# Strassen's seven products in the second product of a fused attention and feed-forward kernel, with masks of four rows moved to GpSimd

## The chip, the cores and the metric

The kernel runs on one core of a Trainium2 chip. The metric is the device time of one execution in microseconds (us), as the median of several runs. A profiled execution comes with a trace of every instruction; its span goes from the first to the last of them.

## The reference

Attention over 8 batch rows, 8 heads, 576 positions and 64 values a head. Four heads see a sliding window of 32 positions, four see every fourth position of the last 128. Its output, 4608 tokens of 512 values, goes through a feed-forward layer:

```python
scores = np.where(masks[None, :, :, :], scores, -1000000000.0)
scores = scores - np.max(scores, axis=-1, keepdims=True)
attn = np.exp(scores)
attn = attn / (np.sum(attn, axis=-1, keepdims=True) + 1e-09)
return np.matmul(attn, v).astype(np.float32)
...
h = x @ w_in
r = np.maximum(h, 0.0)
g = r * r
return (g @ w_out).astype(np.float32)
```

w_in is 512 x 2048, w_out 2048 x 512. Inputs and output are float32; the kernel's matmuls take float16.

## The kernel before, in words

"Row" below is a batch row b (0 to 7), "chunk" is 512 of the 4608 tokens (c = 0 to 8). A chunk needs the attention output of the row with its number and the one before.

*Feed-forward.* The first product (`mm1_tile`, L254) makes one tile of the hidden layer at a time: 128 hidden features by the chunk's 512 tokens, four matmuls (L262) into one PSUM bank. ScalarE takes relu into a tile `rt` of four buffers (L247), VectorE squares it into `g` (L251): 16 tiles a chunk. The second product (`mm2_gen`) has the weights in `g` (128 x 128) and w_out as the moving operand, 512 columns wide: 16 matmuls for each of four groups of 128 tokens (L292), then a copy by ScalarE (L302) and a store from SP's queue (L303). `g` has two buffers, one per chunk. Chunk 0's first product also computes the last 64 tokens of row 0 for chunk 1, so that its second half is 288 columns wide and chunk 1's tiles 448.

*Attention.* Scores (L415 sliding, L429 dilated) go into PSUM pairs, ScalarE takes exp into `AT` (L402), VectorE multiplies by a 0/1 mask (L404). The values product (AV: L470, L484) is normalized by VectorE out of PSUM (L455, L456), transposed by TensorE (L499, L517) and copied by ScalarE into `xT` (L505, L523), a ring of four rows' tokens.

*Loads.* GpSimd's queue loads q and k: `n` (L140) and `dd` (L216). GpSimd copies `n` into token order, `o` (L223); SP stores it to DRAM as `dp` (L229) and loads `dd` and `dp` back transposed into QKTd and QKTp (L241, L237). SP loads v into `sv` and `sd` (L150, L158, L160), and GpSimd casts them to float16 as `vp`, `vd` (L195, L199). `see` (L181) is a one-element copy that makes GpSimd wait for the transposes of a row before it issues the next loads.

*Order.* It is written out by hand. The feed-forward of chunk b - 1 is a generator; the attention of row b calls `pump(n)`, which emits n steps of it. A tile of the first product is two steps; before, the second product has eight steps per group of tokens. For rows 2 to 7 the order before is: `see`, q and k loads for row b + 1, the copy to token order, the transposes, `cast_v`, `load_v` for row b + 1, `pump(24)`, then `attn_scores` with `pump(4)` after each of four scores, then `attn_values` with `pump(2)` after each piece, then the rest of the chunk. Chunks 7 and 8 come after the last row with no attention between. Eight PSUM banks: four (`bank`) are turned over by feed-forward tiles and transposes, four are the two pairs of the attention.

The line numbers in the profile of before are those of the listing.

Of the kernel before, what the change touches and what calls it, by code (L numbers as in the profile page):

```python
# [17 lines left out]
def kernel(  # L18
# [38 lines left out]
    wpool = ctx.enter_context(tc.tile_pool(name="wpool", bufs=1))  # L57
    stg = ctx.enter_context(tc.tile_pool(name="stg", bufs=1))
    natp = ctx.enter_context(tc.tile_pool(name="natp", bufs=2))
    xp = ctx.enter_context(tc.tile_pool(name="xp", bufs=4))  # L60
    gp = ctx.enter_context(tc.tile_pool(name="gp", bufs=2))
    osb = ctx.enter_context(tc.tile_pool(name="osb", bufs=4))
    pspool = ctx.enter_context(tc.tile_pool(name="pspool", bufs=1, space=bass.MemoryType.PSUM))
    dpool = ctx.enter_context(tc.tile_pool(name="dpool", bufs=2, space=bass.MemoryType.DRAM))
# [37 lines left out]
    def w_out_of(ffc):  # L102
        return wo[ffc // 4][:, ffc % 4, :]

    QKTp = [const.tile([P, 2, 2, PADP + S], FP16, name=f"QKTp{r}") for r in range(2)]
    QKTd = [const.tile([P, 2, 2, KPAD + S], FP16, name=f"QKTd{r}") for r in range(2)]
    AT = const.tile([P, 8, 640], FP16, name="AT")
# [27 lines left out]
            )  # L135

    def load_whole_sliding_qk(b):
        n = natp.tile([P, HH, 9, D], FP16, name=f"n{b}", tag="n")
        for i, s in ((1, k), (0, q)):
            nc.gpsimd.dma_start(  # L140
                out=n[64 * i : 64 * (i + 1)],
                in_=s[b, 0:HH].rearrange("h (p j) d -> p h j d", j=9),
            )
        return n
# [97 lines left out]

    def relu_squared(ph, w, outs, name):
        rt = osb.tile([P, TOKC], FP16, name=name, tag="rt")
        nc.scalar.activation(rt[:, 0:w], ph[:, 0:w], ACTF.Relu)  # L247
        o = 0
        for g in outs:
            n = g.shape[1]  # L250
            nc.vector.tensor_mul(g, rt[:, o : o + n], rt[:, o : o + n])  # L251
            o += n

    def mm1_tile(name, ffc, t0, t1, outs):  # L254
        w = t1 - t0
        ph = bank()
        o = t0 % RING
        cut = min(w, RING - o)
        for dmk in range(NDM):
            for a, b, x in ((0, cut, o), (cut, w, 0)):  # L260
                if a < b:
                    nc.tensor.matmul(  # L262
                        ph[:, a:b],
                        w_in_of(dmk, ffc),
                        xT[:, dmk, x : x + b - a],
                        start=(dmk == 0 and a == 0),
                        stop=(dmk == NDM - 1 and b == w),
                    )
            if dmk == 1:
                yield  # L270
        relu_squared(ph, w, outs, f"rt{name}")
        yield

    def mm1_first_gen(g0, g1):

        for f4 in range(0, NFF, 4):
            for ffc in range(f4, f4 + 4):
                yield from mm1_tile(f"0_{ffc}_0", ffc, 0, HALF, [g0[:, ffc, 0:HALF]])
            for ffc in range(f4, f4 + 4):
                yield from mm1_tile(  # L280
                    f"0_{ffc}_1", ffc, HALF, S, [g0[:, ffc, HALF:TOKC], g1[:, ffc, 0:REST]]
                )

    def mm1_gen(c, g):
        o = REST if c == 1 else 0
        for ffc in range(NFF):
            yield from mm1_tile(
                f"{c}_{ffc}", ffc, c * TOKC + o, (c + 1) * TOKC, [g[:, ffc, o:TOKC]]
            )

    def mm2(c, g, po, t, ffc):
        nc.tensor.matmul(  # L292
            po,
            g[:, ffc, t * P : (t + 1) * P],
            w_out_of(ffc),
            start=(ffc == 0),
            stop=(ffc == NFF - 1),
        )
# [3 lines left out]
        nc.scalar.copy(ot, po)  # L302
        nc.sync.dma_start(out=out[(c * 4 + t) * P : (c * 4 + t + 1) * P, :], in_=ot)  # L303

    def mm2_gen(c, g):
        for t in range(TOKC // P):
            po = bank()
            for ffc in range(NFF):
                mm2(c, g, po, t, ffc)
# [5 lines left out]
    def mm2_by_rows_gen(c, g):  # L315
        pos = [
            bank() for t in range(TOKC // P)
        ]
        for f4 in range(0, NFF, 4):
            for t, po in enumerate(pos):  # L320
                for ffc in range(f4, f4 + 4):
                    mm2(c, g, po, t, ffc)
# [6 lines left out]
    def hidden(c):  # L329
        return gp.tile([P, NFF, TOKC], FP16, name=f"g{c}", tag="g")  # L330

    hid = {}

    def moe_gen(c):
        g = hid.pop(c) if c in hid else hidden(c)
        yield from mm1_gen(c, g)
        yield from mm2_gen(c, g)
# [63 lines left out]
    def softmax(u, ps, mask, eng=nc.vector):  # L401
        nc.scalar.activation(AT[:, u, 0:UW], ps[:, :, 0 : UW // 2], ACTF.Exp, scale=scale)  # L402
        if mask is not None:
            eng.tensor_mul(AT[:, u, 0:UW], AT[:, u, 0:UW], mask)  # L404
# [39 lines left out]
    def s_dilated(b, a):  # L444
        tiles = [pair() for t in range(2)]
        for t, ps in enumerate(tiles):
            s_dilated_one(b, a, t, ps)
        for t, ps in enumerate(tiles):
            softmax(4 + 2 * a + t, ps, maskd)

    def normalize(b, what, pav, w):
        x = xp.tile([QB, 2, HH, D], FP16, name=f"x{b}_{what}", tag="x")
# [72 lines left out]
            py[:, 0:UW].rearrange("x (c r i) -> x c i r", c=2, r=DIL),  # L525
        )

    def attn_scores(b, gap):
        for hp in range(2):
            s_sliding(b, hp)  # L530
            pump(gap)
        for a in range(2):
            s_dilated(b, a)
            pump(gap)

    def attn_values(b, gap, wide=False):
        xs = []
        for mp in range(3):
# [18 lines left out]


    ns0 = [stg.tile([P, 2, 9 * D], FP16, name=f"ns0_{hp}") for hp in range(2)]
    nd0 = natp.tile([P, 36 * D], FP16, name="nd0", tag="nd")  # L560
# [121 lines left out]
    xs = [av_sliding(0, mp) for mp in range(2)]  # L682
    x_dilated(0, 0, ys, True)
    x_sliding(0, 0, xs, True)
    g0, g1 = hidden(0), hidden(1)
    hid[1] = g1
    pairs[:] = [2, 3]
    pending.append(mm1_first_gen(g0, g1))
    pump(2)
    zs = [av_dilated(0, 1, 0)]  # L690
    pump(2)
# [5 lines left out]
    x_sliding(0, 1, xs, True)  # L697
    k_pads(1)
    v_ones(1)
    ns1 = natp.tile([P, HH, 9 * D], FP16, name="ns1", tag="n")  # L700
    nd1 = natp.tile([P, 36 * D], FP16, name="nd1", tag="nd")
    for i, src in ((1, k), (0, q)):
        nc.gpsimd.dma_start(
            out=ns1[64 * i : 64 * (i + 1)],
# [19 lines left out]
    o = in_token_order(2, n)  # L724
    transpose_dilated(2, dd)
    transpose_sliding(2, keep_sliding_qk(2, o))
    pending.append(mm2_by_rows_gen(0, g0))
    pump(4)
    t_sliding(1, ns1, 0)
    pump(2)  # L730
# [64 lines left out]
```

## Time and profile before

| what | value |
|---|---|
| median of 3 runs | 318.48 us (318.02 to 320.24) |
| the profiled execution's own time | 317.65 us |
| its span | 315.5 us |
| mean granted clock of TensorE | 0.993 |
| copy of an output tile by ScalarE (L302) | 0.585 us each, 36 of them |
| masks on VectorE (L404) | 56, mean 581 ns (dilated) and 486 ns (sliding) |
| a row and its chunk in the middle, 94.75 to 127.11 us of the span | 32.36 us |
| a chunk with no attention, 256.70 to 284.33 us | 27.63 us |

A line of a group reads: line of the kernel, engine, operation, what it writes <- what it reads, shapes, count | busy us in total, mean ns of one | idle us of the engine before it, and what ended the idle time. PE is TensorE's matmuls, PEld its weight loads, DVE VectorE, ACT ScalarE, POOL GpSimd. In a timeline: start and length in us, engine, line, operation, count of instructions merged into the line, and in brackets the idle time before them. In a line of a window: its bounds and length, then busy us and count of PE, PEld, DVE, ACT and POOL, the granted clock of TensorE, the DMA share and GB/s.

### The profile page before, as it was taken

What the parts mean: (1) busy time and instruction counts of PE and PEld (TensorE: products, weight loads), DVE (VectorE), ACT (ScalarE), POOL (GpSimd) and SP (SyncE); (2) the same over time, 40 slices, a digit from 0 to 9 for tenths busy, and PEclk for the clock granted to TensorE, in tenths of its full rate; (3) what the DMA queues carried; (4) which work ended last, traced back from release to release, by engine and by line L of the source; (5) the groups of instructions that cost most, each with busy time, mean ns of one, the idle gap of its engine ahead of it and who ended that gap; (6) DMA issues with size and microseconds to landing.
All of it is one profiled execution on the core that took longest, in us unless ns stands there. A gap on an engine that the chain in (4) does not pass through costs nothing.

```text
span 315.5 us, 6596 instructions
## 1 busy us (share of the span) xinstructions
PE 303.0 (96%) x2628; PEld 174.7 (55%) x2628; DVE 160.6 (51%) x378; ACT 170.7 (54%) x301; POOL 77.4 (25%) x120
## 2 busy tenths in 40 slices
PE   4988999999999999999999999999999999999995
PEld 3657945565455555555589555555554555445542
DVE  7456757547734974586435652575256524203400
ACT  2647855578336843684368535763577256316611
POOL 5492017203602903533422440040000000000000
PEclk9989999999999999999999999999999999999999
DMA  6999979689979999999978965781100110010011
GB/s 117 235 196 212 214 163 241 139 217 221 202 189 219 273 182 211 292 185 190 239 202 183 191 171 136 169 198 55 68 2 2 66 69 1 31 69 35 0 66 66
DMA packets 72782, 46.69 MB, mean 148 GB/s; under 512 B 54384, under 2 KB 65904, under 8 KB 72560
## 3 DMA queue, kind: packets, MB, share of 16 engines
q1 hardware_dynamic: 65504, 32.65, 42.5%
q0 software_dynamic: 7248, 13.63, 24.4%
q8 instruction: 20, 0.33, 0.4%
q14 instruction: 10, 0.08, 0.1%
HBM read 39.85 MB, written 16.52 MB: 179 GB/s over the span
## 4 chain that ended last, share of the span: by engine, by line
PE 88%; DMA 5%; SPq 1%; POOL 1%; ACT 1%; DVE 1%; issue 1%; POOLq 0%; DVEq 0%
PE PS L292 38%; PE PS L262 38%; PE PS L484 3%; DMA sv<-in_v_dram 3%; DMA ns<-in_q_dram 2%; PE PS L470 2%; PE PS L415 2%; PE PS L429 1%; PE PS L499 1%; PE PS L517 1%; SPq L150 1%; DVE x_p L456 1%; PE PS L359 1%; POOL ns L125 1%; PE PS L408 0%
## 5 line engine op out<-in xcount | busy, mean ns | idle before, releaser
L292 PE MATMUL PS<-wo,g 128*128 128x512 f16 x576 | 140.5, 379 | 0.0
L262 PE MATMUL PS<-xT,wi 128*128 128x512 f16 (+3 forms) x704 | 130.3, 343 | 1.5 <-ACT xT L505 1.5
L251 DVE TENSOR_TENSOR g<-rt 128x512 f16<-128x512 f16 (+4 forms) x176 | 71.8, 421 | 91.4 <-ACT rt L247 89.3
L247 ACT ACTIVATE rt<-PS 128x512 f16<-128x512 f32 (+2 forms) x160 | 88.8, 556 | 33.9 <-PE PS L262 31.4
L262 PEld LDWEIGHTS <-wi 128*128 128x128 f16 x704 | 78.5, 114 | 46.6 <-issue 0.9
L292 PEld LDWEIGHTS <-g 128*128 128x128 f16 x576 | 49.8, 97 | 46.5
L302 ACT COPY ot<-PS 128x512 f32<-128x512 f32 x36 | 21.1, 585 | 51.7 <-PE PS L292 51.7
L402 ACT ACTIVATE AT<-PS 128x576 f16<-128x576 f32 x64 | 38.3, 650 | 8.6 <-PE PS L429 5.7
L505 ACT COPY xT<-PS 128x576 f16<-128x576 f16 x16 | 10.2, 639 | 28.7 <-PE PS L499 28.7
L199 POOL CAST vd<-sd 128x512 f16<-128x512 f32 x32 | 20.3, 662 | 13.1 <-DMA sd<-in_v_dram 13.0
L195 POOL CAST vp<-sv 128x512 f16<-128x512 f32 x24 | 16.4, 696 | 28.0 <-DMA sv<-in_v_dram 27.6
L456 DVE TENSOR_TENSOR x_d<-PS,rcp_d 72x512 f16<-72x512 f32 x32 | 22.0, 686 | 1.1
L223 POOL COPY o<-n 128x2304 f16<-128x2304 f16 x6 | 12.8, 2136 | 28.9 <-DMA n<-in_q_dram 28.9
L404 DVE TENSOR_TENSOR AT<-AT,maskd 128x576 f16<-128x576 f16 x28 | 15.7, 581 | 6.1 <-ACT AT L402 4.6
L456 DVE TENSOR_TENSOR x_p<-PS,rcp_p 96x512 f16<-96x512 f32 x24 | 16.5, 686 | 0.8
L455 DVE RECIPROCAL rcp_d<-PS 72x8 f32<-72x8 f32 x32 | 6.5, 202 | 20.3 <-PE PS L484 19.6
L484 PEld LDWEIGHTS <-AT 128*128 128x128 f16 x256 | 12.5, 101 | 7.6 <-DVE x_d L456 0.8
L404 DVE TENSOR_TENSOR AT<-AT,maskp 128x576 f16<-128x576 f16 x28 | 13.5, 486 | 4.4 <-ACT AT L402 2.2
L523 ACT COPY xT<-PS 128x576 f16<-128x576 f16 x16 | 10.2, 639 | 8.9 <-PE PS L517 8.9
L484 PE MATMUL PS<-vd,AT 128*128 128x65 f16 x256 | 14.0, 199 | 0.0
L470 PEld LDWEIGHTS <-AT 128*128 128x128 f16 x192 | 9.6, 102 | 6.3 <-issue 1.2
L181 POOL COPY look<-QKTp 1x1 f16<-1x1 f16 x5 | 1.2, 232 | 48.1 <-DMA QKTp<-dp 48.1
(63 smaller groups left out, 132.2 us busy)
## 6 DMA issues: line engine op xcount, KB each, us to landing
out_dram<-ot SPq DMA_DIRECT2D x36, 256.0 KB, 2.6
sv<-in_v_dram SPq DMA_DIRECT2D x40, 128.0 KB, 4.5
sd<-in_v_dram SPq DMA_DIRECT2D x8, 512.0 KB, 9.9
dp<-o SPq DMA_DIRECT2D x12, 288.0 KB, 3.8
sd<-in_v_dram SPq DMA_DIRECT2D x8, 288.0 KB
wo<-in_moe_w_out_dram POOLq DMA_DIRECT2D x4, 512.0 KB, 13.2
n<-in_k_dram POOLq DMA_DIRECT2D x6, 288.0 KB, 5.3
n<-in_q_dram POOLq DMA_DIRECT2D x6, 288.0 KB, 6.8
```

The source lines that it names most:

```text
L195: nc.gpsimd.tensor_copy(vp[b % 2][:, m : m + 2, :, 0:D], sv[:, m : m + 2, :, :])
L199: nc.gpsimd.tensor_copy(vd[b % 2][:, t, c : c + 2, :, 0:D], sd[:, t, :, D * c : D * (c + 2)].rearrange("p h (c d) -> p c h d", d=D),)
L247: nc.scalar.activation(rt[:, 0:w], ph[:, 0:w], ACTF.Relu)
L251: nc.vector.tensor_mul(g, rt[:, o : o + n], rt[:, o : o + n])
L262: nc.tensor.matmul(ph[:, a:b], w_in_of(dmk, ffc), xT[:, dmk, x : x + b - a], start=(dmk == 0 and a == 0), stop=(dmk == NDM - 1 and b == w),)
L292: nc.tensor.matmul(po, g[:, ffc, t * P : (t + 1) * P], w_out_of(ffc), start=(ffc == 0), stop=(ffc == NFF - 1),)
L302: nc.scalar.copy(ot, po)
L402: nc.scalar.activation(AT[:, u, 0:UW], ps[:, :, 0 : UW // 2], ACTF.Exp, scale=scale)
L404: eng.tensor_mul(AT[:, u, 0:UW], AT[:, u, 0:UW], mask)
L456: nc.vector.tensor_tensor(out=x[0:w], in0=pv[:, :, :, 0:D], in1=rcp[0:w].unsqueeze(3).to_broadcast([w, 2, HH, D]), op=ALU.mult,)
L470: nc.tensor.matmul(pav[:, i, h * (D + 2) : h * (D + 2) + D + 1], AT[:, 2 * (h // 2) + m // 3, off : off + P], vp[b % 2][:, m, h, 0 : D + 1 ...
L484: nc.tensor.matmul(pav[:, e, h * (D + 2) : h * (D + 2) + D + 1], AT[:, 4 + 2 * a + t, off : off + P], vd[b % 2][:, t, 2 * a + e, h, 0 : D ...
```

## The change

For chunks 2 to 8 the second product is done by Strassen's scheme in Winograd's form. `g` and w_out are cut into quarters; seven products of quarters, each 2 x 8 matmuls with 256 columns, fill one PSUM bank each. VectorE makes four sums of quarters of `g` (S1 to S4) while the first product goes on, two hidden features of each half at a time, and seven additions out of PSUM; GpSimd makes four sums of quarters of w_out (T1 to T4) once. Stores go out by quarters of 256 tokens by 256 values. The tiles of the first product are taken in the order 0, 8, 1, 9, ..., 7, 15. `g` has one buffer, chunk 0 no longer computes for chunk 1, and `n` has one buffer; nd shares its buffers with `o`. The masks of rows 4 to 7 are done by GpSimd. In the loop over rows the copy to token order, the transposes and the loads of v come after the scores; `cast_v` comes after the scores in rows 2 and 3; other counts go to `pump`. A Strassen product is four steps.

```diff
-    gp = ctx.enter_context(tc.tile_pool(name="gp", bufs=2))
+    n1p = ctx.enter_context(tc.tile_pool(name="n1p", bufs=1))
...
+    g = wpool.tile([P, NFF, TOKC], FP16, name="g")
+    HF = NFF // 2
+    HT = TOKC // 2
+    S1, S2, S3, S4 = (wpool.tile([P, HF, HT], FP16, name=f"S{i}") for i in range(1, 5))
+    T1, T2, T3, T4 = (wpool.tile([P, HF, HT], FP16, name=f"T{i}") for i in range(1, 5))
...
-        n = natp.tile([P, HH, 9, D], FP16, name=f"n{b}", tag="n")
+        n = n1p.tile([P, HH, 9, D], FP16, name=f"n{b}", tag="n")
...
+    def sum_w_out(upper):
+
+        for j in range(2):
+            f = slice(4 * j, 4 * j + 4)
+            b11, b12 = wo[j][:, :, 0:HT], wo[j][:, :, HT:DM]
+            b21, b22 = wo[2 + j][:, :, 0:HT], wo[2 + j][:, :, HT:DM]
+            if upper:
+                nc.gpsimd.tensor_sub(T1[:, f, :], b12, b11)
+            else:
+                nc.gpsimd.tensor_sub(T3[:, f, :], b22, b12)
+                nc.gpsimd.tensor_sub(T2[:, f, :], b22, T1[:, f, :])
+                nc.gpsimd.tensor_sub(T4[:, f, :], b21, T2[:, f, :])
+
+    def first_quarters(j):
+        f = slice(j, j + 2)
+        nc.vector.tensor_sub(S3[:, f, :], g[:, f, 0:HT], g[:, f, HT:TOKC])
+
+    def all_quarters(j):
+        f, h = slice(j, j + 2), slice(HF + j, HF + j + 2)
+        nc.vector.tensor_add(S1[:, f, :], g[:, f, HT:TOKC], g[:, h, HT:TOKC])
+        nc.vector.tensor_sub(S2[:, f, :], S1[:, f, :], g[:, f, 0:HT])
+        nc.vector.tensor_sub(S4[:, f, :], g[:, h, 0:HT], S2[:, f, :])
+
+    def mm1_sums_gen(c):
+        for j in range(HF):
+            for ffc in (j, HF + j):
+                yield from mm1_tile(f"{c}_{ffc}", ffc, c * TOKC, (c + 1) * TOKC, g[:, ffc, :])
+                if j % 2 == 1:
+                    (first_quarters if ffc == j else all_quarters)(j - 1)
+                yield
+
+    def product(po, lhs, rhs):
+        for t in range(2):
+            for j in range(HF):
+                nc.tensor.matmul(
+                    po[:, HT * t : HT * (t + 1)],
+                    lhs(j)[:, t * P : (t + 1) * P],
+                    rhs(j),
+                    start=j == 0,
+                    stop=j == HF - 1,
+                )
+                if j == 3:
+                    yield
+            if t == 0:
+                yield
+
+    def seven_gen(c):
...
+        po = bank()
+        yield from product(po, a(0, 0), b(0, 0))
+        s1 = new("s1", "s1")
+        nc.scalar.copy(s1, two(po))
+        yield
+        p7 = bank()
+        yield from product(p7, s(S3), s(T3))
+        yield
+        po = bank()
+        yield from product(po, s(S2), s(T2))
+        u2, t7 = new("u2", "u2"), new("t7", "t7")
+        nc.vector.tensor_add(u2, two(po), s1)
+        nc.vector.tensor_add(t7, two(p7), u2)
+        yield
+        po = bank()
+        yield from product(po, a(0, 1), b(1, 0))
+        c11 = new("c11", "ot")
+        nc.vector.tensor_add(c11, two(po), s1)
+        keep(0, 0, c11)
...
-    def s_sliding(b, hp):
+    def s_sliding(b, hp, eng=nc.vector):
...
-            softmax(2 * hp + half, ps, maskp)
+            softmax(2 * hp + half, ps, maskp, eng)
...
     for b in range(2, B):
-        pending.append(moe_gen(b - 1))
+        pending.append(moe_gen(b - 1) if b == 2 else moe_seven_gen(b - 1))
+        eng = nc.vector if b < 4 else nc.gpsimd
         if b + 1 < B:
             see(QKTp[b % 2][0:1, 0, 0, PADP : PADP + 1])
             n, dd = load_whole_sliding_qk(b + 1), keep_dilated_qk(b + 1)
+        if b > 3:
+            cast_v(b)
+        pump({2: 24, 3: 12}.get(b, 8))
+        s_sliding(b, 0, eng)
+        pump(4 if b == 2 else 6)
+        s_sliding(b, 1, eng)
+        pump({2: 4, 3: 6}.get(b, 8))
+        s_dilated(b, 0, eng)
+        pump({2: 4, 3: 6}.get(b, 8))
+        s_dilated(b, 1, eng)
+        if b < 4:
+            cast_v(b)
+        if b + 1 < B:
             o = in_token_order(b + 1, n)
             transpose_dilated(b + 1, dd)
             transpose_sliding(b + 1, keep_sliding_qk(b + 1, o))
-        cast_v(b)
-        if b + 1 < B:
             load_v(b + 1)
-        pump(24)
-        attn_scores(b, 4)
+        pump(4)
         attn_values(b, 2)
         pump(1000)
     for c in range(B - 1, NTOKC):
-        pending.append(moe_gen(c))
+        pending.append(moe_seven_gen(c))
```

Here `a(i, k)` is the quarter of `g` with tokens i and hidden features k, `b(i, k)` that of w_out. The three products left out are S1 T1, a(1, 1) T4 and S4 b(1, 1), in this order; they are followed by the additions of c22 and v5, of c21, and of c12, each out of the bank of its product.

More of the change, by code (lines that the diff above doesn't have):

```diff
@@ L59 @@
     natp = ctx.enter_context(tc.tile_pool(name="natp", bufs=2))
+    n1p = ctx.enter_context(tc.tile_pool(name="n1p", bufs=1))
     xp = ctx.enter_context(tc.tile_pool(name="xp", bufs=4))
-    gp = ctx.enter_context(tc.tile_pool(name="gp", bufs=2))
+    sump = ctx.enter_context(tc.tile_pool(name="sump", bufs=1))
     osb = ctx.enter_context(tc.tile_pool(name="osb", bufs=4))
@@ L241, in transpose_dilated, with mm1_tile @@
             nc.sync.dma_start_transpose(out=QKTd[b % 2][:, i, :, KPAD:], in_=dd[i])
[L245 to L254, printed above, removed]
+    def mm1_tile(name, ffc, t0, t1, into):
         w = t1 - t0
@@ L270, in mm1_tile, with mm1_first_gen, mm1_gen, mm2 @@
                 yield
-        relu_squared(ph, w, outs, f"rt{name}")
-        yield
-    def mm1_first_gen(g0, g1):
+        rt = osb.tile([P, TOKC], FP16, name=f"rt{name}", tag="rt")
+        nc.scalar.activation(rt[:, 0:w], ph[:, 0:w], ACTF.Relu)
+        nc.vector.tensor_mul(into, rt[:, 0:w], rt[:, 0:w])
+    def mm1_first_gen():
         for f4 in range(0, NFF, 4):
[L277 to L285, printed above, removed]
+            for t0, t1 in ((0, HALF), (HALF, TOKC)):
+                for ffc in range(f4, f4 + 4):
+                    yield from mm1_tile(f"0_{ffc}_{t0}", ffc, t0, t1, g[:, ffc, t0:t1])
+                    yield
+    def mm1_gen(c):
         for ffc in range(NFF):
[L287 to L291, printed above, removed]
+            yield from mm1_tile(f"{c}_{ffc}", ffc, c * TOKC, (c + 1) * TOKC, g[:, ffc, :])
+            yield
+    def mm2(po, t, ffc):
         nc.tensor.matmul(
@@ L303, in store, with mm2_gen @@
         nc.sync.dma_start(out=out[(c * 4 + t) * P : (c * 4 + t + 1) * P, :], in_=ot)
-    def mm2_gen(c, g):
+    def mm2_gen(c):
         for t in range(TOKC // P):
@@ L308, in mm2_gen @@
             for ffc in range(NFF):
-                mm2(c, g, po, t, ffc)
+                mm2(po, t, ffc)
                 if ffc % 2 == 1 and ffc < NFF - 1:
@@ L313, in mm2_gen, with mm2_by_rows_gen @@
             yield
[L315 to L318, printed above, removed]
+    def mm2_by_rows_gen(c):
+        pos = [bank() for t in range(TOKC // P)]
         for f4 in range(0, NFF, 4):
@@ L321, in mm2_by_rows_gen @@
                 for ffc in range(f4, f4 + 4):
-                    mm2(c, g, po, t, ffc)
+                    mm2(po, t, ffc)
                     if ffc % 2 == 1 and ffc < NFF - 1:
@@ L327, in mm2_by_rows_gen @@
                     yield
-    def hidden(c):
-        return gp.tile([P, NFF, TOKC], FP16, name=f"g{c}", tag="g")
-    hid = {}
-    def moe_gen(c):
-        g = hid.pop(c) if c in hid else hidden(c)
-        yield from mm1_gen(c, g)
-        yield from mm2_gen(c, g)
+    def sum_w_out(upper):
[9 more added lines that the diff above has]
+                nc.gpsimd.tensor_sub(T4[:, f, :], b21, T2[:, f, :])
@@ new lines, in first_quarters @@
+    def first_quarters(j):
[9 more added lines that the diff above has]
+            for ffc in (j, HF + j):
+                yield from mm1_tile(f"{c}_{ffc}", ffc, c * TOKC, (c + 1) * TOKC, g[:, ffc, :])
+                if j % 2 == 1:
+                    (first_quarters if ffc == j else all_quarters)(j - 1)
+                yield
@@ new lines, in product, with a, b, s @@
+    def product(po, lhs, rhs):
[13 more added lines that the diff above has]
+    def seven_gen(c):
+        def a(i, k):
+            return lambda j: g[:, HF * k + j, HT * i : HT * (i + 1)]
+        def b(i, k):
+            return lambda j: wo[2 * i + j // 4][:, j % 4, HT * k : HT * (k + 1)]
+        def s(t):
+            return lambda j: t[:, j, :]
+        def new(name, tag):
+            return osb.tile([P, 2, HT], FP32, name=f"{name}{c}", tag=tag, bufs=1 if tag != "ot" else 4)
+        def keep(i, k, o):
+            nc.sync.dma_start(
+                out=out[c * TOKC + HT * i : c * TOKC + HT * (i + 1), HT * k : HT * (k + 1)]
+                .rearrange("(t p) m -> p t m", p=P),
+                in_=o,
+            )
+        two = lambda p_: p_.rearrange("p (t m) -> p t m", t=2)
+        po = bank()
[5 more added lines that the diff above has]
+        yield from product(p7, s(S3), s(T3))
+        yield
+        po = bank()
[3 more added lines that the diff above has]
+        nc.vector.tensor_add(t7, two(p7), u2)
+        yield
+        po = bank()
[3 more added lines that the diff above has]
+        keep(0, 0, c11)
+        yield
+        po = bank()
+        yield from product(po, s(S1), s(T1))
+        c22, v5 = new("c22", "ot"), new("v5", "s1")
+        nc.vector.tensor_add(c22, two(po), t7)
+        nc.vector.tensor_add(v5, two(po), u2)
+        keep(1, 1, c22)
+        yield
+        po = bank()
+        yield from product(po, a(1, 1), s(T4))
+        c21 = new("c21", "ot")
+        nc.vector.tensor_add(c21, two(po), t7)
+        keep(1, 0, c21)
+        yield
+        po = bank()
+        yield from product(po, s(S4), b(1, 1))
+        c12 = new("c12", "ot")
+        nc.vector.tensor_add(c12, two(po), v5)
+        keep(0, 1, c12)
+        yield
@@ L339, with moe_seven_gen @@
+    def moe_gen(c):
+        yield from mm1_gen(c)
+        yield from mm2_gen(c)
+    def moe_seven_gen(c):
+        yield from mm1_sums_gen(c)
+        yield from seven_gen(c)
     pending: list = []
@@ L441, in s_sliding, with s_dilated @@
         for half, ps in enumerate(tiles):
-            softmax(2 * hp + half, ps, maskp)
-    def s_dilated(b, a):
+            softmax(2 * hp + half, ps, maskp, eng)
+    def s_dilated(b, a, eng=nc.vector):
         tiles = [pair() for t in range(2)]
@@ L448, in s_dilated @@
         for t, ps in enumerate(tiles):
-            softmax(4 + 2 * a + t, ps, maskd)
+            softmax(4 + 2 * a + t, ps, maskd, eng)
     def normalize(b, what, pav, w):
@@ L526, in x_dilated @@
         )
[L528 to L534, printed above, removed]
     def attn_values(b, gap, wide=False):
@@ L559 @@
     ns0 = [stg.tile([P, 2, 9 * D], FP16, name=f"ns0_{hp}") for hp in range(2)]
-    nd0 = natp.tile([P, 36 * D], FP16, name="nd0", tag="nd")
+    nd0 = natp.tile([P, 36 * D], FP16, name="nd0", tag="o")
     reli = const.tile([P, QB], I16, name="reli")
@@ L684 @@
     x_sliding(0, 0, xs, True)
-    g0, g1 = hidden(0), hidden(1)
-    hid[1] = g1
     pairs[:] = [2, 3]
-    pending.append(mm1_first_gen(g0, g1))
+    pending.append(mm1_first_gen())
     pump(2)
@@ L699 @@
     v_ones(1)
-    ns1 = natp.tile([P, HH, 9 * D], FP16, name="ns1", tag="n")
-    nd1 = natp.tile([P, 36 * D], FP16, name="nd1", tag="nd")
+    ns1 = n1p.tile([P, HH, 9 * D], FP16, name="ns1", tag="n")
+    nd1 = natp.tile([P, 36 * D], FP16, name="nd1", tag="o")
     for i, src in ((1, k), (0, q)):
@@ L709 @@
     load_w_out(3)
+    sum_w_out(True)
     see(wo[2][0:1, 0, 0:1])
@@ L726 @@
     transpose_sliding(2, keep_sliding_qk(2, o))
-    pending.append(mm2_by_rows_gen(0, g0))
+    pending.append(mm2_by_rows_gen(0))
     pump(4)
@@ L745 @@
     load_v(2)
+    sum_w_out(False)
     for b in range(2, B):
-        pending.append(moe_gen(b - 1))
+        pending.append(moe_gen(b - 1) if b == 2 else moe_seven_gen(b - 1))
+        eng = nc.vector if b < 4 else nc.gpsimd
         if b + 1 < B:
```

## The prediction

> **What bounds the kernel now.** I read the page first (busy shares, the slices), then the chain of waits in order of time, then the groups with shapes kept apart, and last the timelines and single lines of VectorE and GpSimd where the change adds work to them.
>
> ```profile
> PE 303.0 (96%) x2628; PEld 174.7 (55%) x2628; DVE 160.6 (51%) x378; ACT 170.7 (54%) x301; POOL 77.4 (25%) x120
> ...
> PE   4988999999999999999999999999999999999995
> ```
> TensorE is busy in every slice from the third on; the other engines have half of their time free. So a matmul less is time less, as long as nothing makes TensorE wait.
>
> ```profile
> 159.47 10.48 PE PS L262 x96
> ...
> 284.33 13.81 PE PS L262 x64
> 298.14 13.83 PE PS L292 x64
> 312.00 0.58 ACT ot L302
> ```
> The chain (start, length, what) is nearly one row of matmuls. A second product of a chunk, 64 matmuls of 512 columns, takes 13.83 us: 216 ns each. The 96 matmuls at 159.47 are 256 columns wide (the chunk that wraps around the ring of xT), each with a weight load of its own, and take 109.2 ns each: half the width is half the time.
>
> ```profile
> L251 DVE TENSOR_TENSOR g<-rt x16: 424/426/426, 285.9 to 298.8; 128x512 f16<-128x512 f16 x16
> ```
> ```profile
> L251 DVE TENSOR_TENSOR g<-rt x6: 824/826/1914, 103.2 to 109.6; 128x512 f16<-128x512 f16 x6
> ```
> ```profile
> 102.71 2.10 POOL L223 COPY o<-n 128x2304 f16<-128x2304 f16 x1 [5.38 <-DMA n<-in_q_dram]
> 104.76 2.31 POOL L195 CAST vp<-sv 128x512 f16<-128x512 f32 x3
> ```
> ```profile
> L456 DVE TENSOR_TENSOR x_d<-PS,rcp_d x18: 685/686/687, 59.6 to 188.3; 72x512 f16<-72x512 f32 x18
> L456 DVE TENSOR_TENSOR x_p<-PS,rcp_p x15: 686/686/687, 81.6 to 213.9; 96x512 f16<-96x512 f32 x15
> ```
> This decides my forecast. The same squaring (minimum/median/maximum in ns) takes 426 with GpSimd quiet and 824 to 1914 while GpSimd works. It began at 103.18 inside GpSimd's 2.10 us copy and ended at 105.09, 0.28 after that copy's end: it did not run slower, it stood still. After it one squaring gets through per GpSimd cast. An operation of VectorE that reads PSUM (L456) keeps its 686 ns whatever GpSimd does.
>
> ```profile
> L676 POOL TENSOR_TENSOR AT<-AT,maskd 128x576 f16<-128x576 f16 x2 | 2.5, 1281 | 0.0
> ```
> ```profile
> 20.90:24.40 3.50, 3.50 (x32) 2.61 (x29) 2.79 (x9) 1.13 (x3) 3.50 (x7) 0.51 1.15 214
> ```
> Two masks already run on GpSimd, 1.28 us each, 1.24 from start to start, where VectorE has nothing to do that could be held. The last line is a stretch at half clock (0.51) after one in which TensorE had been busy 1.84 of 3.4 us: 3.5 us of work at half speed, 1.7 us lost.
>
> **The change, part by part.** The profiled execution took 317.65 us (span 315.5), 0.83 below the median of 318.48; the sum is made against 317.65.
>
> Matmuls. Per chunk 64 at 216 ns (13.82 us) become 7 x 2 x 8 = 112 at 109.2 ns (12.23): 1.59 us less, seven chunks, -11.1 us. The row has exactly this shape, so I see no reason for another price; if the load of 128 weights (114 ns mean in L262) set the pace, 112 x 114 ns would leave 1.05 us a chunk, -7.4.
>
> First product of chunks 0 and 1. 64 columns move from 64 matmuls of chunk 0 to those of chunk 1: 1.7 us each way (64 x 27 ns, from 216 against 189), 0 together; +1.7 if the early part waits for its loads instead.
>
> GpSimd's eight sums of w_out. At 1.24 us per 576 elements, 2.2 us each. Two lie in the 12.3 us in which GpSimd waits for w_out, six (13.3 us) in the 12.4 us in which it waits for the sliding q and k of row 2, so the next loads are issued 1 us later. They hold squarings of chunk 1, but four rt buffers and four banks let TensorE run eight tiles ahead. 0; at most +1.
>
> ScalarE loses three of four output copies a chunk (3 x 0.58 us) and was not on the chain: 0. The last copy, 0.58, becomes a VectorE addition out of PSUM, by L456 0.69: +0.1. The seven additions a chunk (4.8 us) and the seven normalizations (7 x 0.89) need 11 of the 15.6 us of the second product with its attention matmuls, each bank is wanted four products later, and neither is held by GpSimd: 0. The one buffer for n makes the load of row 2 wait for transposes that end at 43.9; it was issued at 48.2: 0.
>
> VectorE's sums of g. Per four tiles of the first product there are four squarings and four sums of the same size. Squarings back to back start 0.335 us apart (two in 0.75 at 111.07); one that needs the result before it takes 0.426 + 0.03: 4 x 0.335 + 4 x 0.456 = 3.16 us, for 3.45 us of tiles. It fits, barely. In the order of the list g[7], which the eighth matmul of the first Strassen product reads, is VectorE's 27th operation: 10.6 us of work alone. In chunks 7 and 8 no attention runs and nothing is held: 0. What TensorE wants, in us from the chunk's start: 16 tiles x 0.863 + 4 scores x 0.365 = 15.27, and 7 x 0.109 more, 16.04.
>
> Row 3 (chunk 2): masks still on VectorE, six of them ahead of g[7] at 0.5 us; the seven casts, each letting one operation through in 0.75 us instead of 0.39 (+2.5), and the copy (+1.85), which now comes after them, fall into the first product. First squaring at 1.5 (tile 0.86 and relu): 1.5 + 10.6 + 3.0 + 2.5 + 1.85 = 19.45, TensorE waits 3.4 us; 0 if casts and copy come later, as they may.
>
> Rows 4 to 7 (chunks 3 to 6): the masks go to GpSimd. No row shows a GpSimd operation with two inputs beside such a VectorE operation. The bounds are 0 and the full hold that casts and copy show; I take the hold, as 1.24 us of GpSimd reading and writing SBUF is nearest to them. Then one VectorE operation passes per 1.24 + 0.19 us (0.19 is what a cast, 0.56 alone, grows to 0.75), instead of per 0.39: 1.04 lost, eight masks 8.3. The casts land before the chunk starts. The copy moved behind the masks costs 1.85 again. Sum: 1.5 + 10.6 + 0.9 (VectorE waiting for tiles until the first mask comes at 4.7) + 8.3 + 1.85 = 23.2: TensorE stands 7.2 us at its eighth matmul in rows 4, 5 and 6, and 5.3 in row 7, which has no copy. Behind that matmul wait AV, its transposes and everything else of TensorE. Low end: the last two masks and the copy come after g[7] and hold S2 of the third product instead; 4.6 us.
>
> The Trainium skill, "SBUF — State Buffer", section "Who interferes with whom", has the pair of ports that VectorE and GpSimd share as an exclusive lock that whoever is first keeps for its whole instruction. It speaks against this change, and agrees with the 1914 ns. By it the masks hold fully and the sum is the one below; by the casts and the copy alone, which need not speak for masks, it would lie anywhere between 310 and that.
>
> Half clock after such a gap: 1.7 us each in rows 4 to 7, 6.8; between 0 and twice that.
>
> The moved queue work (copy, q and k transposes and v loads behind the scores): with masks ending at 18.9 in a row of 31 us, copy to 21.0, dp stores and their landing 3.5, transposes 2.7 and 3.4 to land: 30.7, wanted at 30.8 + 3.45. 0, and the longer rows give it more slack.
>
> Sum: 317.65 - 11.1 + 0.1 + 3.4 + 3 x 7.2 + 5.3 + 6.8 = 343.75, say 344.
>
> **The rivals.** *Faster: masks on GpSimd do not hold VectorE.* Then g[7] is ready at 1.5 + 10.6 + 0.9 + 1.85 = 14.9, before 16.04, and the time is 306.7 + 3.4 (row 3) = 310, or 306.7 without that wait. It turns at a hold of (16.04 - 14.9) / 8 = 0.15 us a mask. For it: no row shows this pair. Against it: every cast and copy that met such an operation held it.
> *GpSimd and SP as a loop.* v's loads follow the copy, casts follow the loads, masks the casts. If v lands late (sd took 9.9 us), casts end 12 us into the next row, masks three and four come about 1 us late for AV, and this grows: up to 2 us in four rows on top of 310: 311 to 318. The landing times speak for it, the slack above against.
> *Part of the hold.* VectorE gets two operations in between masks, or the masks come when it has little to do: half of the forecast's waits, no half clock, 314 to 325.
>
> **How the numbers follow.** The forecast has 0.66, with its own range 325 (4 x 4.6 on 306.7) to 358 (344 and both further half clocks, 6.8 and 1.7 in row 3, 1.7 and 1 of the early parts, a few tenths a row for late normalizations). No hold has 0.20, the loop 0.06, part of the hold 0.08. About 1% is what a measurement of this kernel tells from no change, that is 315.3 to 321.7. Faster: 0.20 and a little of the loop, 0.21; same: the rest of the loop and part of the last, 0.06; slower 0.73. The range of 312 to 358 leaves out most of "no hold" and a little above.
>
> **What would show it.** Right: the Strassen matmuls 109 ns apart; S and g operations of VectorE at over 1.2 us in rows 4 to 7 and at 0.43 in chunks 7 and 8, which take 26 us each instead of 27.6; idle TensorE in front of the first Strassen product of chunks 3 to 6 ended by VectorE's g; clock digits under 9 there. Wrong: masks on GpSimd beside VectorE operations of 0.43 us, TensorE idle for DMA or GpSimd, or 256-column matmuls over 114 ns.

## The result, and the profile after

The changed kernel took 357.22 us (median of 4 runs, 356.15 to 358.63) beside 318.37 us for the kernel before on the same chip: a ratio of 1.1216, with a 95% interval of 1.116 to 1.1272. The prediction was 344.0 in a range of 312 to 358. The profiled execution took 356.53 us, with a span of 354.8.

The page of the kernel after: the engines' busy time, then two rows of its 40 slices, TensorE's busy tenths and the granted clock.

```profile
PE 305.0 (86%) x2964; PEld 211.5 (60%) x2964; DVE 258.7 (73%) x491; ACT 154.6 (44%) x280; POOL 138.9 (39%) x160
...
PE   4968989999997899838996589947899589999995
...
PEclk9989999999999899958999699997999799999999
```

VectorE's busy time went from 160.6 to 258.7 us, GpSimd's from 77.4 to 138.9, and there are four dents in TensorE's row (the 3, 5, 4 and 5 from slice 18 on), each beside a clock digit of 5 to 7 or one slice ahead of it: rows 4 to 7, once each.

The end of the chain of waits of after (start, length, what):

```profile
298.80 13.81 PE PS L262 x64
312.62 12.23 PE PS L359 x112
324.84 13.81 PE PS L262 x64
338.66 12.24 PE PS L359 x112
350.92 0.69 DVE c L430
```

A Strassen second product takes 12.23 us, 109.2 ns a matmul, and chunks 7 and 8 take 26.04 and 26.08 us where they took 27.63 and 27.67. The gain is there, as predicted, where no attention runs. The rows with attention lost it and more. Their windows, one for each of rows 3 to 7 (bounds and length, busy us and count of PE, PEld, DVE, ACT, POOL, then clock, DMA share, GB/s):

```profile
96.05:132.95 36.90, 32.81 (x318) 22.52 (x316) 29.65 (x60) 17.18 (x30) 15.10 (x23) 0.95 1.02 218
132.95:175.47 42.52, 34.38 (x318) 23.58 (x317) 33.90 (x53) 16.27 (x29) 19.07 (x19) 0.88 0.59 132
175.47:217.45 41.98, 33.61 (x381) 29.67 (x380) 34.13 (x53) 16.17 (x29) 21.51 (x23) 0.92 0.67 131
217.45:258.91 41.46, 32.98 (x318) 22.73 (x316) 33.59 (x53) 16.17 (x29) 19.06 (x18) 0.92 0.58 128
258.91:298.80 39.89, 33.93 (x317) 23.33 (x316) 31.32 (x53) 16.27 (x29) 11.11 (x9) 0.91 0.08 28
```

Before, such a row took 32.36 us at clock 1.00. Row 4 (the second line) in detail. First TensorE's timeline around the start of its second product; the bracket is the idle time before a line and what ended it:

```profile
154.16 0.40 PE L359 MATMUL PS<-wo,g 128*128 128x256 f16 x1 [3.75 <-DVE g L273]
156.74 0.40 PE L359 MATMUL PS<-wo,g 128*128 128x256 f16 x1 [2.18 <-DVE g L273]
...
167.03 1.03 PE L359 MATMUL PS<-wo,g 128*128 128x256 f16 x8 [1.32 <-DVE t L406]
```

What VectorE did in the first of these gaps, and GpSimd beside it:

```profile
151.27 1.43 DVE L346 TENSOR_TENSOR S<-g,S 128x512 f16<-128x512 f16 x1
152.62 4.06 DVE L273 TENSOR_TENSOR g<-rt 128x512 f16<-128x512 f16 x3
```
```profile
151.14 2.68 POOL L507 TENSOR_TENSOR AT<-AT,maskd 128x576 f16<-128x576 f16 x2 [2.57 <-ACT AT L505]
153.77 2.30 POOL L232 COPY o<-n 128x2304 f16<-128x2304 f16 x1
```

Two masks and the copy, 151.14 to 156.07, let three VectorE operations through that take 0.42 us elsewhere; the fourth, at 0.41 us again, ends 0.6 us after the copy. The squarings of these tiles were wanted by then. Operations of VectorE that read PSUM kept their time, as before: the additions (L430) take 0.69 us in the chain above, and the normalizations 0.686 us in all rows.

### The profile page after: what moved, and what is told of

Read it like the earlier page. It is cut to its first block, busy times and chain, and to the rows that moved or that the text cites. A ratio compares the mean times of both kernels' runs of the same rounds, so it can differ in the third digit from the quotient of the medians.

```text
span 354.8 us, 7408 instructions
## 1 busy us (share of the span) xinstructions
PE 305.0 (86%) x2964; PEld 211.5 (60%) x2964; DVE 258.7 (73%) x491; ACT 154.6 (44%) x280; POOL 138.9 (39%) x160
## 4 chain that ended last, share of the span: by engine, by line
PE 58%; DVE 32%; DMA 4%; ACT 2%; issue 1%; POOL 1%; POOLq 0%; ACTq 0%
PE PS L359 24%; PE PS L262 18%; DVE g L273 15%; PE PS L288 8%; DVE S L346 5%; DVE S L345 3%; DVE S L344 3%; PE PS L587 2%; DMA wi<-in_moe_w_in_dram 2%; PE PS L573 2%; DMA sd<-in_v_dram 2%; DVE S L340 2%; ACT rt L272 1%; DVE x_d L559 1%; PE PS L620 1%
## 5 line engine op out<-in xcount | busy, mean ns | idle before, releaser
L262 PE MATMUL PS<-xT,wi 128*128 128x512 f16 (+3 forms) x704 | 132.2, 343 | 3.1 <-ACT rt L272 1.2
L273 DVE TENSOR_TENSOR g<-rt 128x512 f16<-128x512 f16 (+2 forms) x160 | 92.1, 600 | 28.3 <-ACT rt L272 26.8
L262 PEld LDWEIGHTS <-wi 128*128 128x128 f16 x704 | 76.4, 114 | 47.2 <-issue 2.4
L359 PE MATMUL PS<-wo,g 128*128 128x256 f16 x224 | 35.5, 304 | 35.0 <-DVE g L273 24.6
L359 PEld LDWEIGHTS <-g 128*128 128x128 f16 x336 | 33.4, 104 | 45.0 <-DVE g L273 32.3
L359 PEld LDWEIGHTS <-S 128*128 128x128 f16 x448 | 43.3, 101 | 5.6
L359 PE MATMUL PS<-T,S 128*128 128x256 f16 x336 | 45.1, 284 | 0.0
L288 PE MATMUL PS<-wo,g 128*128 128x512 f16 x128 | 32.8, 379 | 0.0
L507 POOL TENSOR_TENSOR AT<-AT,maskd 128x576 f16<-128x576 f16 x16 | 21.8, 1383 | 19.1 <-ACT AT L505 19.1
L507 POOL TENSOR_TENSOR AT<-AT,maskp 128x576 f16<-128x576 f16 x16 | 22.6, 1434 | 6.2 <-ACT AT L505 6.2
L346 DVE TENSOR_TENSOR S<-g,S 128x512 f16<-128x512 f16 x28 | 22.9, 820 | 1.0
L345 DVE TENSOR_TENSOR S<-S,g 128x512 f16<-128x512 f16 x28 | 17.5, 625 | 1.0
```

What stands on the lines that cost most here:

```text
L262: nc.tensor.matmul(ph[:, a:b], w_in_of(dmk, ffc), xT[:, dmk, x : x + b - a], start=(dmk == 0 and a == 0), stop=(dmk == NDM - 1 and b == w),)
L273: nc.vector.tensor_mul(into, rt[:, 0:w], rt[:, 0:w])
L288: nc.tensor.matmul(po, g[:, ffc, t * P : (t + 1) * P], w_out_of(ffc), start=(ffc == 0), stop=(ffc == NFF - 1),)
L345: nc.vector.tensor_sub(S2[:, f, :], S1[:, f, :], g[:, f, 0:HT])
L346: nc.vector.tensor_sub(S4[:, f, :], g[:, h, 0:HT], S2[:, f, :])
L359: nc.tensor.matmul(po[:, HT * t : HT * (t + 1)], lhs(j)[:, t * P : (t + 1) * P], rhs(j), start=j == 0, stop=j == HF - 1,)
```

## The experiments

**1. The masks back on VectorE.**

```diff
-        eng = nc.vector if b < 4 else nc.gpsimd
+        eng = nc.vector
```

> The changed kernel with the masks of rows 4 to 7 on VectorE again. My theory (a mask on GpSimd holds every VectorE operation with two SBUF inputs for its length): g[7] is ready at 1.5 + 10.6 + 6 x 0.5 = 15.1 us, up to 18 with the copy and casts, wanted at 16.04, so TensorE waits 0 to 2 us instead of 4.6 to 7 and the half clock goes: rows 4 to 7 take 32 to 35 us each instead of 39.9 to 42.5, 319 to 331 us, say 325. Rival (VectorE has simply too much to do, and GpSimd helps it): 32 masks x 0.46 = 15 us more on VectorE, 365 to 372 us.

Measured: 329.09 us, ratio to before 1.0329 [1.0274, 1.0384]. One line of the change gives back 28 of the 39 us; rows 5, 6 and 7 fall from 42.0, 41.5 and 39.9 us to 33.4, 34.0 and 32.9, row 4 only to 38.2, since GpSimd's last casts and its copy (2.30 us) still meet its first sums. Three lines of its waits view (us in total, times, longest) show what is left:

```profile
PEld L573 <- DVE x_p L559: 7.1, 5, 3.0
PE PS L359 <- DVE t L406: 6.6, 5, 1.3
...
PE PS L359 <- DVE g L273: 3.7, 4, 2.3
```

The wait for `g` has shrunk. What remains is the values product, which waits for a normalization standing behind VectorE's sums and masks, and five waits of 1.3 us in the Strassen products (experiment 5).

**2. No masks at all in rows 4 to 7.** `if mask is not None` becomes false in these rows.

> The changed kernel with the masks of rows 4 to 7 left out (part of the computation is left out). My theory: nothing holds VectorE but casts and copy, g[7] comes in time, rows 4 to 7 take 30.8 us and the 1.3 us that the fourth product waits for a bank: 318 to 323 us, a little under the run with masks on VectorE. Rival (VectorE's own list of sums and squarings is too long whatever GpSimd does): over 340 us.

Measured: one run, 327.47 us, above the expected band. Rows 4 to 7 take 33.2, 33.4, 33.2 and 32.9 us. In rows 5 to 7 that is little less than with the masks on VectorE (33.4, 34.0 and 32.9), so the masks as a mere amount of work matter little there. Totals hide this in part: row 3, which experiments 1 to 3 leave as it is, took 36.9 us in the first, 39.2 here and 38.9 in the third. The 21 us over the ideal (317.65 - 11.1 = 306.5) have causes besides the masks: even without them a row does not come down to 30.8 us. The bank takes 1.32 us of it, and in rows 4 to 6 TensorE waits some 0.75 us more for a normalization behind VectorE's sums; the line below has these waits, with a longer one in row 3.

```profile
PE PS L573 <- DVE x_p L559: 6.1, 5, 3.4
```

**3. Fills in place of masks.** GpSimd does two fills of the same tile where it did a mask.

```diff
-            eng.tensor_mul(AT[:, u, 0:UW], AT[:, u, 0:UW], mask)
+            if eng is nc.gpsimd:
+                for _ in range(2):
+                    eng.memset(AT[:, u, 0:UW], 1.0)
+            else:
+                eng.tensor_mul(AT[:, u, 0:UW], AT[:, u, 0:UW], mask)
```

> The changed kernel with each GpSimd mask replaced by two GpSimd fills of the same tile with ones (the masks of rows 4 to 7 are left out), about as long together, which write SBUF and read nothing. If a GpSimd operation holds VectorE only when it reads SBUF, as the Trainium skill's SBUF page has it: as without masks, 318 to 323 us, squarings beside fills at 0.43. If any GpSimd operation holds it: 345 to 357 us and squarings at 0.8 and more beside fills.

Measured: one run, 329.23 us, above the first band as experiment 2 was, and far below the second. The timelines of GpSimd and VectorE in row 4:

```profile
140.11 4.67 POOL L509 MEMSET AT<- 128x576 f16 x8
```
```profile
140.49 0.42 DVE L346 TENSOR_TENSOR S<-g,S 128x512 f16<-128x512 f16 x1
140.83 1.15 DVE L273 TENSOR_TENSOR g<-rt 128x512 f16<-128x512 f16 x3
142.01 0.43 DVE L340 TENSOR_TENSOR S<-g 128x512 f16<-128x512 f16 x1
```

GpSimd writes the same tile for 4.67 us without a break, and VectorE's squarings and sums keep their 0.42 us. A GpSimd instruction that only writes holds nothing; one that reads SBUF does. The Trainium skill, "SBUF — State Buffer", section "Who interferes with whom", says just this of a VectorE instruction with two SBUF inputs: that it contends with a GpSimd instruction that reads SBUF, "not with one that only writes it". The runs agree: 0.42 us here, 1.43 under the masks.

**4. The kernel before, with masks of rows 4 to 7 on GpSimd.** The other half of the change is left out.

> The kernel before, with nothing changed but that the masks of rows 4 to 7 are on GpSimd. My theory: the hold shows on squarings beside a mask (over 1.2 us instead of 0.43), but VectorE has 17 of 32 us to do per row, four squarings are left when the first mask comes, and TensorE waits little: 317 to 321 us. Rival (a mask on GpSimd is late in itself, for the values product): 8 masks x 1.28 against 0.46, up to 6 us a row, 325 to 342 us.

Measured: 318.81 us, ratio 1.0012 [0.9981, 1.0042]: no change. The squarings of rows 4 to 6 and the masks, by line (minimum/median/maximum ns):

```profile
L251 DVE TENSOR_TENSOR g<-rt x48: 424/426/1495, 130.8 to 210.0; 128x512 f16<-128x512 f16 x48
```
```profile
L404 POOL TENSOR_TENSOR AT<-AT,maskp x16: 1270/1452/1457, 140.8 to 242.1; 128x576 f16<-128x576 f16 x16
```

The hold is there (1495 against 426) and costs nothing: the scores come after 24 steps, so that in row 4 five of the eight masks start beside the second product (from 144.30 on), and VectorE, which in the kernel before had 20.3 us of work in such a row of 32.4, makes up for it. So moving masks to GpSimd is not slow by itself.

**5. The second and third Strassen product exchanged.** In after, transposes of the attention take banks from the same ring of four as the products, so that the fourth product gets the bank of `p7`, which is held until `t7` is added, after the third.

```diff
-        p7 = bank()
-        yield from product(p7, s(S3), s(T3))
-        yield
         po = bank()
         yield from product(po, s(S2), s(T2))
...
+        p7 = bank()
+        yield from product(p7, s(S3), s(T3))
+        nc.vector.tensor_add(t7, two(p7), u2)
```

> The changed kernel with its second and third Strassen product in the other order (S2 T2 before S3 T3), so that the bank of S3 T3 no longer waits for u2. In the changed kernel the fourth product waits 1.32 us in rows 3 to 7 for VectorE's t7, since the transposes of the attention take two of the four banks in between. My theory: this wait goes and the waits for g[7] stay: 357 - 6.6 = 350.6, 349 to 353 us. Rival (VectorE is late anyway, and the wait only moves to the next product): 355 to 358 us.

Measured: one run, 351.42 us, as expected. No wait of the products for `t` is left in the list of waits, where after had 6.6 us, five times 1.32; those for `g` stay (22.9 us in all, beside 24.6). The gain is not even: row 4 takes 2.1 us less and row 7 2.3, rows 5 and 6 only 0.8 and 0.5, and row 3 takes 1.0 more.

**6. No sums of `g`.** The 16 sums a chunk are left out, four of the seven products run on zeros; the masks stay on GpSimd.

> The changed kernel with its 16 sums of g per chunk left out (S1 to S4 are zeros; part of the computation is left out); masks of rows 4 to 7 stay on GpSimd. My theory (it takes both, a VectorE list that fills the first product and masks that hold it): 15 squarings are left ahead of g[7], eight masks let one of them pass each 1.43 us, and the wait for g[7] is 0 to 2 us: 316 to 324 us. Rival (the masks on GpSimd are late for the values product, or slow in themselves): 335 to 357 us.

Measured: one run, 333.16 us, a miss for the theory as I had put it ("it takes both, sums and masks"). The chain of waits in rows 4 and 5, and two of its waits:

```profile
138.90 11.32 DVE g L273 x8
...
176.67 11.18 DVE g L273 x8
```
```profile
PE PS L357 <- DVE g L273: 11.0, 7, 2.5
PE PS L357 <- DVE t L404: 6.6, 5, 1.3
```

Eight squarings in a row take 1.41 us each, the period of the masks. With the sums as well the time is 24 us longer (357.22 against 333.16). But the seven waits for `g` all lie in rows 3 to 6, and rows 4 to 6 take 37.7 us each; row 7 has its masks on GpSimd too, takes 32.3 us and doesn't wait for `g`. GpSimd in row 4, and the first masks of row 7:

```profile
138.74 5.53 POOL L505 TENSOR_TENSOR AT<-AT,maskp 128x576 f16<-128x576 f16 x4
144.24 5.68 POOL L505 TENSOR_TENSOR AT<-AT,maskd 128x576 f16<-128x576 f16 x4
...
247.89 2.70 POOL L505 TENSOR_TENSOR AT<-AT,maskp 128x576 f16<-128x576 f16 x2 [3.11 <-ACT AT L503]
```

In rows 4 to 6 the masks stand behind casts that wait for v, and come as one block of eight with the copy behind it: such a block slows the first product even if VectorE has nothing else to do. In row 7 they come in pairs, and there is no copy; VectorE catches up in between. There it does take both: row 7 takes 39.9 us with sums and masks, 32.3 with these masks alone, and 32.9 with the sums and the masks on VectorE (experiment 1). In experiment 4 the masks are a block as well; what sets it apart is, as far as these runs show, where the scores stand: after 24 steps instead of 8, most masks meet no squaring. No run moves the scores alone.

**7. A version from these findings.** All masks on VectorE, products exchanged, the sums of w_out on VectorE after row 1, scores after 28 steps and then every 4.

```diff
+        eng = nc.vector
...
-        pump({2: 24, 3: 12}.get(b, 8))
+        pump(24 if b == 2 else 28)
         s_sliding(b, 0, eng)
-        pump(4 if b == 2 else 6)
+        pump(4)
```

> A version for the causes so far: all masks on VectorE, scores of rows 3 to 7 behind 28 steps of the first product with 4 steps in between, so that most masks come when VectorE's sums are done, S2 T2 before S3 T3, and the eight sums of w_out on VectorE after row 1. If the waits for g[7], for the bank and for the held squarings of chunk 0 are what stands between the changed kernel and its 11.1 us of saved matmuls: 306.7 us and up to 6 for copy and casts that still hold VectorE, 307 to 313 us. If not: over 318.

Measured: 320.47 us, ratio 1.0085 [1.0051, 1.0119]; a miss by 7 us or more. Chunks 7 and 8 take 26 us, but row 4 takes 33.4 and not 30.8. The end of that row in its chain:

```profile
163.54 0.68 DVE c L430
164.37 0.70 DVE x_d L559
165.42 12.23 PE PS L262 x112
```

44 steps ahead of the values product and 20 within it are more than the 60 a chunk now has: the last normalization and transposes stand alone at the row's end. And GpSimd's copy (2.29 us) still meets the sums of the first product. Row 3 loses most, with 35.0 us: TensorE waits 1.92 us there for a sum, 0.85 for `g` and 0.99 at its end.

**8. Version 7 with the scores after 24, 3, 3 and 3 steps, and with copy, transposes and v's loads after the values product.**

```diff
+        pump(24)
...
+        pump(3)
+        attn_values(b, 2)
         if b + 1 < B:
             o = in_token_order(b + 1, n)
             transpose_dilated(b + 1, dd)
             transpose_sliding(b + 1, keep_sliding_qk(b + 1, o))
             load_v(b + 1)
```

> The version of the run before this (masks and sums of w_out on VectorE, products 2 and 3 swapped, 320.5 us), with two edits: the copy to token order, the transposes and the loads of v come after the pieces of the values product, where VectorE works out of PSUM and no sum of g is open; and the scores come after 24, 3, 3 and 3 steps, so that 56 of the 60 steps of a chunk are used up by the attention and its end lies beside the last product. Theory (what is left of the 1.4 to 5 us a row over 30.8 is the copy's hold on the sums, some 2 us in rows 3 to 6, and the last normalization, transposes and copy of the attention after the last matmul, 1.5 to 2 us in rows 3 to 7): 308 to 314 us, say 311. Rival (the copy, its stores and transposes, some 9 us in a row, now end too late for the next row's first score, and the next q and k loads with them): 317 us or more, with TensorE's scores waiting for QKTp.

Measured: 323.96 us, ratio 1.0155 [1.0104, 1.0206]; again a miss, and no faster than version 7. The row's end is now covered, but v lands later (chunk 2 starts 3.0 us later, at 99.29, with one wait of 2.83 us for a cast of v), and rows 4 to 7 stay at 32.8 to 33.6 us. Two causes show. The rival came true in part: in rows 4 to 7 a score waits for the transposes into QKTp, 0.36 us in row 4, then 1.07, 1.13 and 0.96.

```profile
PE PS L518 <- DMA QKTp<-dp: 3.5, 4, 1.1
```

The other is VectorE. A part of the chain in row 4:

```profile
148.55 1.15 DVE AT L507 x2
151.42 0.74 DVE AT L507 x2
152.30 0.70 DVE x_p L559
153.48 0.87 PE PS L359 x8
```

From 132.93 to 152.07 us its timeline is an almost unbroken list of 16 squarings, 16 sums and 8 masks, and the normalizations come after it; TensorE waits 0.79 us for a sum and 0.52 for a normalization. By the prediction's prices 4 x 3.16 us of squarings and sums and 8 masks at some 0.5 make 16.6 us, already more than the 15.3 to 16.0 that TensorE wants. Little is held any more (two masks take 1.78 us beside casts, where others take 0.82). That this list alone would be too long is an estimate: in no run does it stand without casts and late transposes beside it.

**9. The same with the seven casts of v on ScalarE, after the second score.**

> The same with the seven casts of v of rows 2 to 7 on ScalarE, after the second score, instead of GpSimd: no GpSimd instruction of those rows then reads SBUF while the sums of g are made. Theory (the casts cost their hold in rows where they meet the sums, 2 to 3 us in row 3, less in the others): 0 to 4 us less than with the copy alone moved, 306 to 312, say 309. Rival (seven casts of some 0.6 us each stand before the relus in ScalarE's list and delay the squarings by as much): the same or up to 4 us more, with TensorE's wait for g back.

Measured: 383.41 us, ratio 1.1963 [1.1876, 1.205]: neither theory. ScalarE's timeline in row 5:

```profile
168.74 0.62 ACT L198 CAST vp<-sv 128x512 f16<-128x512 f32 x1 [1.90 <-DMA sv<-in_v_dram]
174.39 1.14 ACT L198 CAST vd<-sd 128x512 f16<-128x512 f32 x2 [5.03 <-DMA sd<-in_v_dram]
176.72 1.14 ACT L198 CAST vd<-sd 128x512 f16<-128x512 f32 x2 [1.20 <-DMA sd<-in_v_dram]
177.76 1.08 ACT L273 ACTIVATE rt<-PS 128x512 f16<-128x512 f32 x2
```

I had priced the casts by their length and forgotten what they wait for: v's loads, which experiment 8 had made late. On GpSimd such a wait stands in front of nothing urgent; in ScalarE's list the relus and exps of the row stand behind it. With v loaded early it might go otherwise; that was not tried.

**10. Strassen's products in chunks 7 and 8 only.** Masks, order of the rows and second product as before in chunks 1 to 6; the sums of w_out on VectorE after row 7, the products exchanged as in experiment 5.

```diff
-        pending.append(moe_gen(b - 1) if b == 2 else moe_seven_gen(b - 1))
+        pending.append(moe_gen(b - 1))
...
+    sum_w_out(True)
+    sum_w_out(False)
     for c in range(B - 1, NTOKC):
         pending.append(moe_seven_gen(c))
```

> The order of the loop over rows, the masks and the second product of before for chunks 1 to 6; Strassen's products only in chunks 7 and 8, which have no attention beside them; the eight sums of w_out on VectorE after row 7, products 2 and 3 swapped, one buffer for g. Theory (the gain of 1.6 us a chunk is there wherever VectorE has room for the sums of g, and the loss comes from the rows): 3.2 us less than before, less the 0.1 of the last addition, and up to 1.5 more for the one buffer of g and for the sums of w_out, some 6.4 us of VectorE beside the end of row 7: 314.5 to 317, say 315.5, a ratio of 0.988 to 0.997. Rival (the one buffer of g and the early part without chunk 0's help cost as much as two Strassen chunks bring): 318 us or more.

Measured: 315.27 us, ratio 0.9888 [0.9848, 0.9929]: 1.1% faster than the kernel before. Its chain ends:

```profile
256.46 13.81 PE PS L262 x64
270.27 12.23 PE PS L359 x112
282.50 13.81 PE PS L262 x64
296.31 12.24 PE PS L359 x112
308.58 0.69 DVE c L430
```

Chunk 7 starts at 256.46 (before: 256.70), so nothing is lost ahead of it, and the two chunks bring 1.6 us each.

## Why the prediction was right, and where 13 us were missing

The forecast's mechanism held: masks on GpSimd hold VectorE's squarings and sums, `g` comes late, TensorE stands in front of the first Strassen product. Its terms, against the trace of after:

- *Matmuls*: 109.2 ns each, as predicted.
- *Full hold of the masks*: one operation per 1.43 us predicted; a held sum takes 1.38 to 1.52 us in row 4, and the squarings of experiment 6 follow each other every 1.41. The rival without a hold falls with experiment 1. The loop of GpSimd and SP falls with the list of waits of after: none of TensorE's waits for GpSimd or a DMA lies in a row with Strassen's products. "Part of the hold" forecast 314 to 325 and falls with the result.
- *Waits for `g`*: predicted 7.2, 7.2, 7.2 and 5.3 us in rows 4 to 7, 3.4 in row 3; the timeline shows 6.8 (0.89, ended by a relu, ahead of the lines shown, then 3.75 and 2.18), 7.05, 7.2 and 4.6, and 2.8. Two details were off. It is not only the eighth matmul that waits: the seventh stands 3.75 us for g[6] before it, and the eighth 2.18 for g[7]. And the casts of v didn't land before the chunk: two of them run at 135.27 in row 4, four at 177.68 in row 5, beside the first squarings. That the sizes agree so closely is in part luck.
- *The bank wait, costed at 0: the first step that failed.* I wrote that each bank is wanted four products later. But the transposes of the attention take banks from the same ring, and `p7` is not freed by its own product but by the addition after the next. 1.32 us in five rows, 6.6; experiment 5 takes it away and is 5.1 us faster than the profiled execution of after.
- *Half clock, mis-sized.* Predicted 1.7 us a row, from a stretch of 3.5 us at 0.51. In row 4 it lasted longer:

```profile
149.60:157.00 7.40, 1.47 (x10) 0.79 (x9) 7.26 (x9) 2.50 (x5) 4.92 (x3) 0.69 0.00 0
157.00:163.50 6.50, 6.50 (x57) 5.17 (x56) 4.33 (x11) 0.60 (x2) 0.00 (x0) 0.56 0.78 182
163.50:175.47 11.97, 10.65 (x136) 9.65 (x134) 7.34 (x14) 2.54 (x4) 4.33 (x8) 1.00 1.05 214
```

  6.5 us at 0.56 cost 6.5 x 0.44 = 2.9 us, and the seventh and eighth matmul, alone in the gap, a little more. I had copied the row for the loss. The gap before it is longer here (7.4 us against 3.4), but its length alone doesn't set the loss: behind waits of 7.05 and 7.2 us, rows 5 and 6 worked 4.0 and 3.0 us at half clock, row 4 5.9 behind 6.8 and row 7 5.0 behind 4.6. The profile has all changes of the clock in these rows on one grid of 3.41 us (half from 152.42, 196.80, 237.76 and 278.72, full again from 162.66, 203.62, 244.58 and 285.54). Two steps of the grid in row 4 and one in row 6:

```profile
155.83:159.25 3.42, 2.51 (x20) 1.96 (x21) 3.25 (x9) 0.00 (x0) 0.24 (x1) 0.50 0.59 136
159.25:162.66 3.41, 3.41 (x30) 2.66 (x28) 2.05 (x5) 0.58 (x1) 0.00 (x0) 0.50 0.66 161
241.17:244.58 3.41, 3.00 (x27) 2.39 (x28) 3.19 (x9) 0.42 (x1) 0.00 (x0) 0.50 0.69 173
```

  In these four rows half clock ended with the first step in which TensorE worked 3.0 us or more; 2.51 us did not end it. So the loss depends on where on the grid the wait ends. Row 3, which has no half clock in the sum, has a mean clock of 0.95.
- *Sums of w_out, costed at 0, bound +1*: with the first two of them on GpSimd beside chunk 0, chunk 1 starts at 63.69 us; in version 7, which has all eight on VectorE after row 1, it starts at 61.83. That is 1.9 us between two executions; from chunk 0's first matmul of L262 to chunk 1 it took 42.8 to 43.6 us in five runs with the sums on GpSimd and 41.7 to 42.3 in four with them on VectorE, 1.2 less on average. The cover named, eight tiles of lead, was for chunk 1; the first two sums hold squarings of chunk 0. The chain of after has 4.74 us of four squarings at 30.13, and TensorE stands 0.18 and 1.05 us behind them.

Row by row after exceeds the forecast by 1.3 us up to chunk 2, 2.7 in row 3, 2.85, 2.15 and 1.8 in rows 4 to 6 and 2.1 in row 7: 12.9, and the profiled execution missed the sum by 12.8. In row 4 the trace gives for its 2.85: 1.32 of the bank, 1.2 of the clock, the matmuls in the gap at 0.69, 1.47 x 0.31 = 0.5, and -0.4 for the shorter wait; 0.2 stays open. In row 3 the 2.7 are 1.32 of the bank and 0.05 x 32.8 of work = 1.6 of the clock, less 0.6 for the shorter wait; 0.4 stays open, less than the 2.3 us by which this row varied over experiments 1 to 3.

That 357.22 lies in the range at all, 0.8 us under its end, is partly luck. The 6.6 us of the bank had no place in it; they fitted in because the terms that its upper end was made of, 14 us over the sum, came to 6.2.

One thing was not in the forecast at all, because it lies behind the wait: "it fits, barely" was true of squarings and sums alone. With the masks on VectorE the list is some 16.6 us by the same prices, and rows 4 to 7 gain next to nothing from Strassen even in versions 7 and 8 (at best 0.3 us, in row 5 of version 7). That the masks are what makes it too long isn't shown: without any mask (experiment 2) these rows take 32.9 us and more, 1.32 of it for the bank, and a run with neither masks nor that wait is missing.

## What to carry to other kernels

A scheme that trades matmuls for additions is paid by the engine that adds, in the stretch where the additions are due: write that engine's list for one period, with all else that it does there, before counting the matmuls saved. Here the scheme pays 1.6 us a chunk where no attention runs (chunks 7 and 8), and in no version tried more than 0.3 us beside the attention. Work handed to GpSimd is not off VectorE if it reads SBUF; whether that costs depends on what VectorE has open at that moment, so where it stands, and whether it comes in one block, can count for more than how much of it there is. A bank held for a value that is combined later is held past its own product, and whoever else draws from the same ring moves the turn at which it is wanted.

## What the runs showed of the hardware

- A GpSimd instruction that only writes SBUF (fill, 128x576, 0.58 us) doesn't hold a two-input VectorE operation at all; one that reads (mask, 1.28 us alone, 1.45 beside VectorE) let one through per instruction (eight squarings beside eight masks, 1.41 us apart).
- TensorE's clock stayed at 0.56 for 6.5 us of unbroken work after a gap of 7.4 us in which it did 1.47 us of work, nearly twice as long as the 3.5 us seen in the kernel before. Rows 5 and 6, with waits as long, had 4.0 and 3.0 us at half clock: it ended on a grid of 3.41 us, with the first step in which TensorE worked at least 3.0 us.
